# Linear attention and MLP on one core: the denominators, numerators and spreads of batch 1 a slot sooner, and two matmuls moved ahead of a spread

## Chip, cores and metric

One core of one Trainium2 chip. The metric is the device time of one execution in microseconds. "Before" and "changed" are the two kernels.

## The reference, cut

```python
# q, k, v: (8 batches, 8 heads, 576 positions, 64), float32
phi = lambda x: np.where(x > 0, x, np.exp(x) - 1.0) + 1.0
kv  = einsum('bhsd,bhse->bhde', phi(k), v);  z = phi(k).sum(axis=2)
num = einsum('bhsd,bhde->bhse', phi(q), kv)
den = einsum('bhsd,bhd->bhs', phi(q), z)[..., None] + 1e-06
x   = (num / den) as (4608 tokens, 512)
h   = x @ w_in                       # (512, 2048)
out = (h - tanh(h)) @ w_out          # (2048, 512)
```

## The kernel before

Products run in bf16 (the spreads of batch 0 in f32). The 4608 tokens pass through the two MLP products in nine chunks of 512; a batch has 576, so chunk 1 needs the last 64 tokens of batch 0 and 448 of batch 1. Attention of batch 1 is worked in between the matmuls of chunk 0. In chunk 0 the second product is cut into 16 "slots" of four 128x512 matmuls; `s2[n]` lists what is issued behind slot n. The denominators of a batch come out of TensorE as a small tile; VectorE inverts it (`rden`), splits it into bf16 parts (`a_split`), TensorE spreads it over partitions ("spread"), and VectorE multiplies the numerators with it ("scaling"), which gives `xT`, the input of the first product. The "kv matmuls" multiply k and v of a batch (line 177 for batch 1, line 199 for the later ones). One scaling makes one "pair" of heads, and each 128x512 matmul of the first product reads one pair.

```python
def a_scale(b, p, ns, bp, o):                        # a scaling of batch 1 (line 359 of the profile)
    nc.vector.tensor_mul(xT[:, p, S*b:S*b+S]..., ns[:, p]..., bp[:, :, o:o+144]...)
...
b0_spread((0, 2), 0)                                 # batch 0: first spread, banks 4 to 7
b0_scale(0, ns0, 0, 0, 4); b0_scale(0, ns0, 0, 4, 8) # pair 0 in halves (line 244)
b0_scale(2, ns0, 1)                                  # pair 2
b0_num(1, ns0)
def open2():
    b0_spread((1, 3), 2)                             # second spread, the same four banks
    b0_scale(1, ns0, 2); b0_scale(3, ns0, 3)
...
# chunk 0, slots of the second product
s2[4].append(lambda: (a_qphi(1, 1), load_q(2), load_k(2), load_v(2)))
s2[7].append(lambda: (a_qT_pe(1, 0, side), a_kv(1, side), a_qT_pe(1, 1, side)))
s2[8].append(lambda: b0_scale_rest(side))
s2[9].append(lambda: (a_den(1, side), num1(), a_split(1)))
s2[11].append(lambda: spread1(0))                    # 8 small matmuls and the scalings of pairs 0, 1
s2[11].append(lambda: (exp2(qs, q_t, qp_t, "qp", 0), rest2(qs[0])))
s2[12].append(lambda: exp2(qs, q_t, qp_t, "qp", 1))
s2[13].append(lambda: (spread1(1), exp2(ks, k_t, kp_t, "kp", 0), rest2(qs[1]), a_qT_dma(2)))
s2[14].append(lambda: rest2(ks[0]))
...
# chunk 0, first product: (pair, block) in the order of issue
order = [((0, 0), (0, 1)), ((2, 0), (2, 1), (0, 2), (0, 3), (2, 2), (2, 3)),
         [(p, fi) for p in (1, 3) for fi in range(4)]]
for n, part_ in enumerate(order):
    if n == 1:
        open2()
    ...
```

Behind slots 12 to 15 ScalarE copies one finished output bank each ("eviction", line 396), and the `exp2` calls put q's and k's exponentials of batch 2 on ScalarE among them.

## Time and profile before

| | before |
|---|---|
| median of 3 executions | 293.31 us (293.09 to 293.58) |
| span of the profiled one | 291.8 us |
| TensorE, VectorE, ScalarE busy | 98%, 60%, 48% |

TensorE is the bound, but the busy share cannot tell where it waits, since its durations overlap. What tells it is the distance between starts: 0.216 us from one 128x512 matmul to the next in a stream. A clearly longer distance is a wait, with two exceptions: where the tile shape of the matmul changes, 0.306 to 0.312 us is the distance without a wait; and 0.428 to 0.432 us, two beats, is taken for a record missing from the trace.

### The profile page before, as it was taken

What the parts mean: (1) busy time and instruction counts of PE and PEld (TensorE: products, weight loads), DVE (VectorE), ACT (ScalarE), POOL (GpSimd) and SP (SyncE); (2) the same over time, 40 slices, a digit from 0 to 9 for tenths busy, and PEclk for the clock granted to TensorE, in tenths of its full rate; (3) what the DMA queues carried; (4) which work ended last, traced back from release to release, by engine and by line L of the source; (5) the groups of instructions that cost most, each with busy time, mean ns of one, the idle gap of its engine ahead of it and who ended that gap; (6) DMA issues with size and microseconds to landing.
All of it is one profiled execution on the core that took longest, in us unless ns stands there. A gap on an engine that the chain in (4) does not pass through costs nothing.

```text
span 291.8 us, 4505 instructions
## 1 busy us (share of the span) xinstructions
PE 285.5 (98%) x1803; PEld 134.5 (46%) x1803; DVE 175.1 (60%) x266; ACT 139.7 (48%) x168; POOL 33.7 (12%) x56
## 2 busy tenths in 40 slices
PE   8999999999999999999999999999999999999994
PEld 3544464454454444444454444444544444444443
DVE  4759958987468674776478637865581457106600
ACT  4938548846354733465345534751551155126411
POOL 8674030110030003000300030000000000000000
PEclk9999999999999999999999999999999999999999
DMA  7999999997999768965895579666117310130032
GB/s 105 193 202 212 208 206 215 194 183 149 249 158 161 175 128 137 197 146 121 136 223 123 123 139 197 146 138 139 30 38 165 73 36 0 43 83 19 0 74 72
DMA packets 39093, 38.94 MB, mean 133 GB/s; under 512 B 16352, under 2 KB 33824, under 8 KB 38304
## 3 DMA queue, kind: packets, MB, share of 16 engines
q0 software_dynamic: 17568, 18.35, 39.0%
q1 hardware_dynamic: 21344, 20.17, 30.9%
q8 instruction: 14, 0.23, 0.3%
q10 hardware_dynamic: 160, 0.13, 0.1%
q14 instruction: 7, 0.06, 0.1%
HBM read 43.91 MB, written 9.55 MB: 183 GB/s over the span
## 4 chain that ended last, share of the span: by engine, by line
PE 85%; DMA 11%; POOL 2%; issue 1%; DVE 0%; POOLq 0%
PE ps_all L387 39%; PE ps_all L366 38%; DMA v<-in_v_dram 6%; DMA w_in_sb<-in_moe_w_in_dram 3%; PE ps_all L199 2%; DMA kraw<-in_k_dram 2%; PE ps_all L317 2%; PE ps_all L618 1%; PE ps_all L276 1%; POOL v L419 1%; PE ps_all L177 1%; POOL qraw L90 0%; PE ps_all L320 0%; POOL qraw L93 0%; POOL w_out_sb L115 0%
## 5 line engine op out<-in xcount | busy, mean ns | idle before, releaser
L366 PE MATMUL ps_all<-xT,w_in_sb 128*128 128x512 bf16 x574 | 127.6, 379 | 0.0
L387 PE MATMUL ps_all<-w_out_sb,gT 128*128 128x512 bf16 x560 | 127.5, 379 | 0.0
L373 DVE TENSOR_TENSOR gT<-ps_all,th 128x1024 bf16<-128x1024 f32 x64 | 77.9, 1218 | 59.2 <-ACT th L372 59.2
L372 ACT ACTIVATE th<-ps_all 128x1024 f32<-128x1024 f32 x64 | 65.6, 1025 | 57.1 <-PE ps_all L366 46.5
L366 PEld LDWEIGHTS <-w_in_sb 128*128 128x128 bf16 x574 | 55.0, 98 | 66.1 <-issue 0.3
L387 PEld LDWEIGHTS <-gT 128*128 128x128 bf16 x560 | 54.2, 98 | 64.2
L396 ACT COPY osb<-ps_all 128x512 f32<-128x512 f32 (+1 forms) x36 | 20.9, 583 | 71.8 <-PE ps_all L387 52.6
L328 DVE TENSOR_TENSOR xT<-ps_all,rdb 128x512 bf16<-128x512 f32 x24 | 16.5, 691 | 13.7 <-PE ps_all L317 11.2
L134 ACT ACTIVATE e<-qraw 128x1152 bf16<-128x1152 bf16 x16 | 18.5, 1160 | 8.2 <-DMA qraw<-in_q_dram 8.2
L134 ACT ACTIVATE e<-kraw 128x1152 bf16<-128x1152 bf16 x15 | 17.5, 1164 | 0.3 <-DMA kraw<-in_k_dram 0.3
L136 DVE TENSOR_TENSOR qp<-e,r 128x1152 bf16<-128x1152 bf16 x16 | 12.1, 758 | 8.0 <-ACT e L134 7.2
L136 DVE TENSOR_TENSOR kp<-e,r 128x1152 bf16<-128x1152 bf16 x15 | 11.4, 759 | 7.9 <-ACT e L134 6.9
L383 POOL COPY g<-qT 1x1 bf16<-1x1 bf16 x5 | 0.9, 178 | 119.2 <-DMA qT<-qp 119.2
L378 DVE TENSOR_TENSOR gT<-ps_all,th 128x512 bf16<-128x512 f32 x16 | 10.3, 686 | 2.4 <-ACT th L377 1.7
L377 ACT ACTIVATE th<-ps_all 128x512 f32<-128x512 f32 x16 | 9.2, 598 | 4.4 <-PE ps_all L366 3.2
L447 PE MATMUL ps_all<-zero 128*128 128x512 bf16 x29 | 9.2, 480 | 1.2 <-DVE zero L405 1.2
L317 PE MATMUL ps_all<-qT,kz 128*128 128x512 bf16 x28 | 10.1, 379 | 0.0
L135 DVE TENSOR_SCALAR r<-qraw 128x1152 bf16<-128x1152 bf16 x16 | 7.3, 454 | 2.1 <-DMA qraw<-in_q_dram 2.1
L199 PEld LDWEIGHTS <-kp 64*128 64x128 bf16 x216 | 6.4, 94 | 2.5 <-issue 2.1
L285 DVE RECIPROCAL rden<-den 128x144 f32<-128x144 f32 x7 | 7.4, 1053 | 0.2
L199 PE MATMUL ps_all<-vp,kp 64*128 64x136 bf16 x216 | 7.4, 220 | 0.0
L394 DVE COPY osb<-ps_all 128x128 f32<-128x128 f32 x1 | 0.3, 292 | 11.6 <-PE ps_all L618 11.6
(85 smaller groups left out, 123.6 us busy)
## 6 DMA issues: line engine op xcount, KB each, us to landing
out_dram<-osb SPq DMA_DIRECT2D x70, 128.0 KB
rdb<-ds SPq DMA_DIRECT2D x12, 576.0 KB
kraw<-in_k_dram POOLq DMA_DIRECT2D x7, 576.0 KB, 7.1
qraw<-in_q_dram POOLq DMA_DIRECT2D x7, 576.0 KB, 9.1
v<-in_v_dram POOLq DMA_DIRECT2D x7, 576.0 KB, 11.6
w_in_sb<-in_moe_w_in_dram POOLq DMA_DIRECT2D x6, 256.0 KB, 8.7
w_out_sb<-in_moe_w_out_dram POOLq DMA_DIRECT2D x3, 512.0 KB, 14.7
qraw<-in_q_dram POOLq DMA_DIRECT2D x2, 288.0 KB, 4.4
```

Source lines behind the costliest of these rows:

```text
L134: return (lambda: nc.scalar.activation(e, x, AF.Exp), lambda: nc.vector.tensor_scalar(r, x, 0.0, 1.0, ALU.max, ALU.add), lambda: nc.vector ...
L136: lambda: nc.vector.tensor_tensor(y, e, r, ALU.min))
L199: nc.tensor.matmul(ps[hg][:, i, :], kp[r, i, j].rearrange("p h d -> p (h d)"), vp[r, i, j, :], start=(j == 0), stop=(j == J - 1))
L317: nc.tensor.matmul(ps, kz[:, p // 2, p % 2, 0:128], qT[:, p % 2, 0:8, p // 2, :], start=True, stop=True)
L328: nc.vector.tensor_mul(xT[:, p, S * b:S * b + 512].rearrange("p (j t c) -> p j t c", j=8, t=4), ps.rearrange("p j (t c) -> p j t c", t=4), ...
L366: nc.tensor.matmul(h, w_in_sb[:, 2 * (p % 2) + p // 2, fi * 128:(fi + 1) * 128], xT[:, p, c * 512:(c + 1) * 512], start=(n == 0), stop=(n ...
L372: nc.scalar.activation(th, h, AF.Tanh)
L373: nc.vector.tensor_sub(gT[:, fi:fi + 2, :], h, th)
L377: nc.scalar.activation(th, h, AF.Tanh)
L378: nc.vector.tensor_sub(gT[:, fi, :], h, th)
L387: nc.tensor.matmul(o, gT[:, fi, i * 128:(i + 1) * 128], w_out_sb[:, fi, :], start=(fi == 0), stop=(fi == NF - 1))
L396: nc.scalar.copy(osb[:, f0:f1], o[:, f0:f1])
```

## The change

The intent: start the long VectorE chain of batch 1 (invert, split) and its spreads earlier, so that the scalings are done well ahead of chunk 1; and let TensorE do something useful ahead of the second spread of batch 0.

```diff
-            s2[8].append(lambda: b0_scale_rest(side))
-            s2[9].append(lambda: (a_den(1, side), num1(), a_split(1)))
-            s2[11].append(lambda: spread1(0))
+            s2[8].append(lambda: (b0_scale_rest(side), a_den(1, side), num1(), a_split(1)))
+            s2[10].append(lambda: spread1(0))
...
-            s2[11].append(lambda: (exp2(qs, q_t, qp_t, "qp", 0), rest2(qs[0])))
-            s2[12].append(lambda: exp2(qs, q_t, qp_t, "qp", 1))
-            s2[13].append(lambda: (spread1(1), exp2(ks, k_t, kp_t, "kp", 0), rest2(qs[1]), a_qT_dma(2)))
+            s2[11].append(lambda: exp2(qs, q_t, qp_t, "qp", 0))
+            s2[12].append(lambda: (spread1(1), exp2(qs, q_t, qp_t, "qp", 1), rest2(qs[0])))
+            s2[13].append(lambda: (exp2(ks, k_t, kp_t, "kp", 0), rest2(qs[1]), a_qT_dma(2)))
...
-            order = [((0, 0), (0, 1)), ((2, 0), (2, 1), (0, 2), (0, 3), (2, 2), (2, 3)),
+            order = [((0, 0), (0, 1)), ((2, 0), (2, 1)), ((0, 2), (0, 3), (2, 2), (2, 3)),
...
-                if n == 1:
+                if n == 2:
                     open2()
```

The last two edits are part A, the slots are part B.

## The prediction

> **What bounds the kernel now.** I read the page first, then the chain of work that ended last in order of time, then the timeline of each engine around the two places the diff touches (14 to 20 us and 38 to 53 us), and last the start of every matmul in the trace. From the page:
>
> ```profile
> span 291.8 us, 4505 instructions
> PE 285.5 (98%) x1803; PEld 134.5 (46%) x1803; DVE 175.1 (60%) x266; ACT 139.7 (48%) x168; POOL 33.7 (12%) x56
> PE 85%; DMA 11%; POOL 2%; issue 1%; DVE 0%; POOLq 0%
> ```
>
> TensorE is the bound: no other engine is over 60% busy, and the last chain is 85% TensorE. What this change can win is time in which TensorE stands still, not work. In the middle of the span a 128x512 matmul starts every 0.216 us (the durations of 379 ns in the page overlap). So I listed every start later than that: after 52.10 us there is none that waits, only fixed extra gaps of 0.095 us (start to start 0.309 to 0.312 us) where matmuls of another tile shape begin, alike in every batch. Whatever reaches 52.10 us sooner ends sooner, and whatever doesn't, doesn't. Between 17.68 us and 38.4 us TensorE keeps its 0.216 us beat with no wait. So the whole case is decided by a few waits, and by what ends each of them. From the chain, in order of time (start, length, what):
>
> ```profile
> 22.32 16.50 DMA v<-in_v_dram
> 38.83 0.04 issue
> 38.87 1.66 PE ps_all L177 x36
> ```
>
> The reader is to see that the path does not run through TensorE before 38.87 us: it runs through the load of v of batch 1, issued by GpSimd at 22.32 us and landing at 38.82. TensorE had started its last transpose at 38.427; 0.056 for it and 0.095 for the shape change make 38.58, so it stood 0.29 us for that load.
>
> The second place, ScalarE's timeline behind slot 11:
>
> ```profile
> 47.34 1.16 ACT L134 ACTIVATE e<-qraw 128x1152 bf16<-128x1152 bf16 x1 [1.40 <-DMA qraw<-in_q_dram]
> 48.41 0.57 ACT L396 COPY osb<-ps_all 128x512 f32<-128x512 f32 x1
> 48.87 1.16 ACT L134 ACTIVATE e<-qraw 128x1152 bf16<-128x1152 bf16 x1
> 49.94 0.57 ACT L396 COPY osb<-ps_all 128x512 f32<-128x512 f32 x1
> 50.40 1.17 ACT L134 ACTIVATE e<-kraw 128x1152 bf16<-128x1152 bf16 x1
> 51.47 1.07 ACT L396 COPY osb<-ps_all 128x512 f32<-128x512 f32 x2
> ```
>
> ScalarE sits idle 1.40 us until q of batch 2 lands (47.27), then works back to back through three exponentials and the evictions of output banks 0, 1, 2, 3. The eviction of bank 2 starts at 51.47 and ends at 52.05. The ninth matmul of chunk 1 writes that bank, and two narrow cuts of TensorE's timeline show it late:
>
> ```profile
> 51.75 0.38 PE L366 MATMUL ps_all<-xT,w_in_sb 128*128 128x512 bf16 x1
> 52.10 0.38 PE L366 MATMUL ps_all<-xT,w_in_sb 128*128 128x512 bf16 x1
> ```
>
> It starts 0.353 us after its neighbour (51.748 to 52.101) instead of 0.216: 0.137 us of wait, ended by ScalarE, whose time was set by a load.
>
> **What the Trainium skill says.** "PSUM — Partial Sum Buffer", section "PSUM bank collisions raise a hardware error", says accesses must be kept apart by bank and quadrant, not by address. The trace agrees: the second spread of batch 0 writes columns 256 and up of banks 4 to 7, VectorE reads columns below that, and still the spread starts at 17.02, just after VectorE's read of pair 2 ended (16.29 + 0.68 = 16.97). "TensorEngine Tiling (Array Packing)", section "Key Properties", says a change of tiling mode drains TensorE; the 0.095 us extra at each shape change here fits. "TensorE: Matmul & The Clock Gate", section "Back-to-back issue gap", gives N/2.4 + 2.5 ns for isolated matmuls, 216 ns at N = 512, and 131 ns sustained; this trace shows 216 in long streams, so I use 216.
>
> **The change, part A: two matmuls ahead of the second spread.** Nothing is added or removed. Before, TensorE ends the four 128x256 matmuls at 16.64 (last start 16.53 + 0.108) and stands until 17.02 for VectorE's scaling of pair 2. The matmuls (2,0) and (2,1) put there multiply xT of pair 2, which is the output of that same scaling: in the compiled order the wait has simply moved from the spread to matmul (2,0). They start at about 17.02 too and fill nothing. The spread then starts 2 x 0.216 later, plus about 0.1 for the shape change that used to lie inside the wait: 17.55. It takes 0.66 (17.02 to 17.68 before), so TensorE goes on at 18.21 with four matmuls and comes to pair 1 at 18.21 + 0.86 = 19.07. Pair 1 is scaled 1.55 us after the spread starts (before: 17.02 to 17.885 + 0.686 = 18.57), so at 19.10, seen at about 19.15. Before, pair 1 began at 18.985. Part A by itself costs 0 to 0.17 us; early loading of the spread's weights might give back 0.1. Either way it lies ahead of the 0.29 us wait for v at 38.87 and vanishes in it.
>
> **Part B: denominators, numerators and spreads a slot sooner.** In the compiled order one group of four 128x512 matmuls (4 x 0.216 = 0.864 us) moves from ahead of the denominators of batch 1 to behind the last spread. TensorE's work stays equal. From VectorE's timeline:
>
> ```profile
> 42.16 0.42 DVE L263 TENSOR_TENSOR xT<-ps_all,rdb 128x256 bf16<-128x256 f32 x1 [0.37 <-PE ps_all L320]
> 43.40 0.31 DVE L281 TENSOR_SCALAR den<-ps_all 128x144 f32<-128x144 f32 x1 [0.82 <-PE ps_all L276]
> 43.74 1.05 DVE L285 RECIPROCAL rden<-den 128x144 f32<-128x144 f32 x1
> 45.77 0.37 DVE L298 SCALAR_TENSOR_TENSOR w<-t,part,u 128x144 bf16<-128x144 bf16 x1
> ```
>
> From the addition at L281 to the end of w is 46.14 - 43.40 = 2.74 us, reciprocal and splitting included. Before, TensorE was ready for the first spread at 46.09 and got w at 46.195: 0.10 us of wait. After, the denominators' matmuls start at about 42.08 (42.91 - 0.864 + 0.03 for another shape change); VectorE is still in L263, so L281 starts at about 42.55, w is done at 45.29, and the spread can start at 45.35. TensorE arrives 8 matmuls after the numerators, about 43.44 + 1.73 + 0.095 = 45.27. So a wait of 0.08 remains, not zero, because the same eight matmuls lie between numerators and spread as before. Chunk 1 begins at about 50.24 + 0.02.
>
> What B does buy is slack: on VectorE, scalings of pairs 2 and 3 now stand ahead of the q work of batch 2 and end at about 49.3 rather than 50.62. But pair 3 is first needed at 50.885, so the 50.62 was already 0.26 us early. Then TensorE comes to bank 2 at about 51.98, and that bank is free at 52.05 as before: ScalarE's order of instructions is unchanged and its chain starts from a load whose issue (38.81, after the q work of batch 1) TensorE does not set. It starts at 52.10 in both kernels.
>
> **Sum.** A: at most +0.17, hidden by 0.29. B: +0.02, hidden by 0.137. After 52.10: 0. Expected difference 0.0 us, from 293.31 us. I take 293.2, a tenth lower, since other executions may have v and q land earlier, where a little of the sooner scalings could show.
>
> **The rivals.**
> 1. *The scalings were sometimes late.* Before, scalings 2 and 3 stood on VectorE behind work that waits for the q load; a later landing would stop TensorE at pair 3, and B removes that. Against: pair 3 follows the landing by 3.4 us (50.67 - 47.27), the bank 2 eviction by 4.8, and TensorE needs 1.1 us between the two, so the eviction is the later one in any case. Worth 0 to 0.3 us.
> 2. *Loads land sooner in most executions than in the profiled one.* Then neither wait hides anything, A's cost of up to 0.17 and B's 0.02 show, and the time is up to 293.5.
> 3. *A new wait in B:* numerator banks 6 and 7 are reused only 0.1 to 0.2 us after VectorE has read them (bank 7: read ends 42.86, next matmul at about 43.0). If VectorE is 0.2 late, TensorE is too: 0.1 to 0.2 us, mostly swallowed at 52.10.
> 4. *A real gain* of the size of the removed waits: 0.38 + 0.10 us, to 292.8. For it speaks only the intent; against it the two load-bound waits.
>
> **Range and chances.** Three executions before spread over 0.49 us (293.09 to 293.58), as landings vary. Taking rivals 2 and 4 as ends, 292.8 to 293.7. A change of 2% is 5.9 us; all of TensorE's idle time is 291.8 - 285.5 = 6.3 us, nearly all of it before the first matmuls and after the last. So within 2% is all but certain.
>
> **What would show it.** In the changed kernel's trace: matmul (2,0) starting at about 17.02 and the second spread after 17.4; the start of the kv matmuls of batch 1 still set by v's load near 38.9; the first spread near 45.35 with a small VectorE wait; the last two scalings of batch 1 done by 49.4; a late matmul near 52.1 behind the eviction of bank 2. The prediction is wrong if loads land elsewhere (a landing 1 us off moves the end by as much), or if chunk 1's ninth matmul no longer waits.

## The result

| | before | changed |
|---|---|---|
| median of 5 executions | 293.38 us (293.09 to 293.61) | 293.50 us (293.18 to 293.90) |
| ratio, 95% interval | | 1.0004 (0.9989 to 1.0018) |
| span of the profiled one | 291.8 us | 291.7 us |

A ratio is the mean time of one kernel's fast runs over that of the other's of the same rounds, so not quite the ratio of the medians. The time is the same within the noise, and inside the predicted range. From the changed kernel's page:

```profile
span 291.7 us, 4505 instructions
...
PE 285.7 (98%) x1803; PEld 134.8 (46%) x1803; DVE 174.9 (60%) x266; ACT 139.9 (48%) x168; POOL 33.8 (12%) x56
...
PE 90%; DMA 5%; POOL 1%; DVE 1%; ACT 1%; issue 1%; SPq 0%; DVEq 0%; POOLq 0%
```

The busy times say nothing. The chain that ended last does: DMA's share fell from 11% to 5%. Its pieces in order of time (start, length, what):

```profile
15.85 1.36 DVE xT L244 x3
17.21 0.04 issue
17.25 0.59 PE ps_all L366 x2
17.84 0.66 PE ps_all L240 x16
18.50 13.12 PE ps_all L366 x60
31.62 6.91 PE ps_all L387 x32
38.53 0.50 PE ps_all L164 x9
39.03 1.59 PE ps_all L177 x36
```

In this execution the path runs through TensorE without a break; the load of v of batch 1, which carried it before, is no longer in this stretch. v landed at 38.59 us, 0.37 us before TensorE came to the kv matmuls (L177, first start 38.962).

Part A, on TensorE's timeline (start, length, engine, line, operation, output and inputs, shape, count, and in brackets the idle time ahead with what ended it), before:

```profile
16.09 0.71 PE L580 MATMUL ps_all<-xT,w_in_sb 128*128 128x256 bf16 x4
...
17.02 0.73 PE L240 MATMUL ps_all<-rden,sel 32*128 32x128 f32 x16 [0.22 <-DVE xT L244]
...
17.68 8.59 PE L366 MATMUL ps_all<-xT,w_in_sb 128*128 128x512 bf16 x39
```

and changed:

```profile
17.25 0.59 PE L366 MATMUL ps_all<-xT,w_in_sb 128*128 128x512 bf16 x2 [0.22 <-DVE xT L244]
17.77 0.73 PE L240 MATMUL ps_all<-rden,sel 32*128 32x128 f32 x16
18.43 1.32 PE L366 MATMUL ps_all<-xT,w_in_sb 128*128 128x512 bf16 x5
```

The wait in brackets is the same 0.22 us, for the same VectorE scaling; it has moved from the spread to the two matmuls. Nothing was filled. VectorE's scalings of batch 0, before and changed:

```profile
15.62 1.35 DVE L244 TENSOR_TENSOR xT<-ns,ps_all 128x256 bf16<-128x256 f32 x3 [0.50 <-PE ps_all L240]
17.89 1.29 DVE L244 TENSOR_TENSOR xT<-ns,ps_all 128x512 bf16<-128x512 f32 x2 [0.92 <-PE ps_all L240]
```

```profile
15.85 1.35 DVE L244 TENSOR_TENSOR xT<-ns,ps_all 128x256 bf16<-128x256 f32 x3 [0.50 <-PE ps_all L240]
18.63 1.29 DVE L244 TENSOR_TENSOR xT<-ns,ps_all 128x512 bf16<-128x512 f32 x2 [1.44 <-PE ps_all L240]
```

VectorE now idles 1.44 us instead of 0.92 ahead of pairs 1 and 3, because the spread comes later.

Part B, VectorE's last two scalings of batch 1, before and changed:

```profile
49.21 1.41 DVE L359 TENSOR_TENSOR xT<-ns,ps_all 128x576 bf16<-128x576 f32 x2
```

```profile
47.85 1.42 DVE L359 TENSOR_TENSOR xT<-ns,ps_all 128x576 bf16<-128x576 f32 x2 [0.58 <-PE ps_all L354]
```

They end at 49.27 instead of 50.62 us, as intended. ScalarE's chain in the changed kernel:

```profile
46.58 1.16 ACT L134 ACTIVATE e<-qraw 128x1152 bf16<-128x1152 bf16 x1 [1.42 <-DMA qraw<-in_q_dram]
...
50.72 1.07 ACT L396 COPY osb<-ps_all 128x512 f32<-128x512 f32 x2
```

and chunk 1's matmuls on TensorE:

```profile
50.33 4.05 PE L366 MATMUL ps_all<-xT,w_in_sb 128*128 128x512 bf16 x18
```

q of batch 2 landed 0.75 us earlier than in the trace of before, so bank 2 was evicted by 51.30, and the ninth matmul of chunk 1 did not wait: it started at 52.055, 0.215 us after its neighbour.

**The ledger.** The start of one matmul can be compared between traces only as a distance from another, because the beginning itself jitters: the first scaling of batch 0 started at 15.62 us in one trace and 15.85 in the other, with nothing changed ahead of it. So I cut the span at five marks and compare the pieces:

| piece (us) | before | changed | difference |
|---|---|---|---|
| start to first scaling of batch 0 | 15.617 | 15.845 | +0.228 |
| to the first matmul of pair 1, chunk 0 (A) | 3.368 | 3.529 | +0.161 |
| to the first kv matmul of batch 1 (wait for v) | 19.885 | 19.588 | -0.297 |
| to the first matmul of chunk 1 (B) | 11.367 | 11.367 | 0.000 |
| to the first kv matmul of batch 2 (wait for bank 2) | 8.001 | 7.866 | -0.135 |
| to the end | 233.558 | 233.544 | -0.014 |
| sum | 291.796 | 291.739 | -0.057 |

One trace each: the second and fourth rows are the change, the first, third and fifth could be loads that landed differently. So the small sum does not show yet that A's 0.161 us was hidden. The experiments are to tell that.

### The profile page after: what moved, and what is told of

Same layout as the page of the kernel before. It is cut to its first block, busy times and chain, and to the rows that moved or that the text cites. A ratio compares the mean times of both kernels' runs of the same rounds, so it can differ in the third digit from the quotient of the medians.

```text
span 291.7 us, 4505 instructions
## 1 busy us (share of the span) xinstructions
PE 285.7 (98%) x1803; PEld 134.8 (46%) x1803; DVE 174.9 (60%) x266; ACT 139.9 (48%) x168; POOL 33.8 (12%) x56
## 4 chain that ended last, share of the span: by engine, by line
PE 90%; DMA 5%; POOL 1%; DVE 1%; ACT 1%; issue 1%; SPq 0%; DVEq 0%; POOLq 0%
PE ps_all L366 43%; PE ps_all L387 39%; DMA v<-in_v_dram 3%; DMA out_dram<-osb 2%; PE ps_all L199 2%; PE ps_all L317 2%; PE ps_all L276 1%; ACT osb L396 1%; PE ps_all L177 1%; POOL kraw L90 0%; PE ps_all L240 0%; SPq L401 0%; DVE xT L244 0%; POOL qraw L90 0%; PE ps_all L221 0%
```

## The experiments

Theory: part A costs 0.16 us on TensorE, part B nothing; the end is set by the later of TensorE's own work and two loads (v of batch 1 at the kv matmuls, q of batch 2 through the eviction of bank 2), so part of A is hidden, and B's slack lies where nothing waits. Rivals: B gains what A loses; or A pays. Runs of one group shared a chip and the runs of before.

### Part A alone

```diff
-            order = [((0, 0), (0, 1)), ((2, 0), (2, 1), (0, 2), (0, 3), (2, 2), (2, 3)),
+            order = [((0, 0), (0, 1)), ((2, 0), (2, 1)), ((0, 2), (0, 3), (2, 2), (2, 3)),
-                if n == 1:
+                if n == 2:
```

> Part A alone (two matmuls of pair 2 ahead of the second spread of batch 0), the slots as before. My theory: in the trace pair 1's first matmul of chunk 0 starts 0.1 to 0.2 us later, counted from the first scaling of batch 0 (before 18.985 - 15.617 = 3.37 us, here 3.5 to 3.55), with a small VectorE wait; at the end 0.0 to +0.2 us, according to how much of it the wait for v of batch 1 hides. Rival 'A pays': the same distance shrinks by up to 0.38 us and the time falls by 0.1 to 0.4 us.

Measured: median 293.53 us (before in these rounds 293.50), ratio 1.0000 (0.9988 to 1.0013). First scaling to pair 1: 3.529 us, to the nanosecond the changed kernel's. The wait for v in this trace was 0.30 us (0.450 between starts less the 0.152 that the last transpose and the shape change need). A loses 0.161 us; "A pays" falls.

### Part B alone

The slots of the changed kernel, with `order` and `open2` as before.

> Part B alone (denominators, numerators and spreads a slot sooner), the order of chunk 0 as before. My theory: from the first kv matmul of batch 1 to the first matmul of chunk 1 TensorE needs 11.37 us as before, within 0.05, a wait of about 0.1 us before the first spread stays; time within 0.2 us of before. Rival 'B gains what A loses': this distance shrinks by 0.1 to 0.2 us, and this kernel is 0.1 to 0.3 us faster than before and than the changed one.

Measured: median 293.28 us, ratio 0.9993 (0.9980 to 1.0005). From kv to chunk 1 11.368 us, as before (11.367). "B gains what A loses" falls on that distance. The end of the chain on VectorE's timeline and the spread on TensorE's show why the wait for `w` stays:

```profile
44.64 0.37 DVE L298 SCALAR_TENSOR_TENSOR w<-t,part,u 128x144 bf16<-128x144 bf16 x1
```

```profile
45.06 0.30 PE L354 MATMUL ps_all<-w,sel 32*128 32x144 bf16 x8
```

`w` is ready at 45.01 and the spread starts at 45.06, 0.417 us after the matmul ahead of it (before: 0.415). Both ends moved by the same slot, so the wait between them (0.417 less 0.312) is the same 0.10 us.

### Before and changed once more

Both kernels unedited, as a control and for second traces.

> The kernel before, unchanged, as a control and for a second trace. All theories: ratio 1.000 within 0.002. My theory of the loads: when v of batch 1 lands after the last transpose of the first half of q of batch 1, TensorE stands; in this trace that wait is somewhere between 0 and 0.5 us, the distances on TensorE between the waits are the same as in the first trace within 0.02 us.

> The changed kernel, unchanged, for a second trace and on the same chip as the control. All theories: within 0.2% of before. My theory: distance from the first scaling of batch 0 to pair 1's first matmul again 3.53 us (before 3.37), from the first kv matmul to chunk 1 again 11.37 us.

Measured: before again 293.49 us, ratio 0.9995 (0.9982 to 1.0007); changed again 293.51, ratio 0.9999 (0.9985 to 1.0013). So the noise of such a comparison is some 0.13%, 0.38 us, more than A costs: only the distances inside the traces can settle this. They repeat: first scaling to pair 1 3.369 and 3.529 us, kv to chunk 1 11.367 and 11.368. What does not repeat is the loads: the wait at the kv matmuls was 0.26 us in the second trace of before and 0.14 in that of the changed kernel, the wait for bank 2 0 and 0.19. In the first pair it was the other way round for bank 2 (0.14 before, none changed). So the fifth row of the ledger does not follow the change: the wait at bank 2 comes and goes in both kernels. The third row, the wait for v, depends both on when v lands and on how late TensorE arrives.

### Part A made larger

```diff
-            order = [((0, 0), (0, 1)), ((2, 0), (2, 1), (0, 2), (0, 3), (2, 2), (2, 3)),
+            order = [((0, 0), (0, 1)), ((2, 0), (2, 1), (0, 2), (0, 3), (2, 2), (2, 3)), (),
-                if n == 1:
+                if n == 2:
```

> Part A made larger: all six matmuls (two of pair 2, four more) ahead of the second spread, the rest as before. My theory: the spread starts 4 matmuls later than in part A, 0.87 us, and pair 1 waits for its scaling; scaling 0 to pair 1's first matmul is 3.529 + 0.865 = 4.39 us (before 3.37), so 1.03 us lost there; 0.15 to 0.3 us of it is hidden by the wait for v; the end is 0.6 to 1.0 us later, ratio 1.002 to 1.0035. Rival 'the loads hide it': the wait for v takes it up wholly and the time stays within 0.2 us. Rival 'A pays': the distance stays below 3.37.

Measured: median 294.20 us against 293.35, ratio 1.0035 (1.0022 to 1.0049), that is about 1.0 us slower. First scaling to pair 1: 4.393 us, 1.03 more than before, where 4.39 was expected. (One matmul record ahead of it is missing in this trace; the time is read from the matmul's own record.)

```profile
18.32 0.73 PE L240 MATMUL ps_all<-rden,sel 32*128 32x128 f32 x16
19.93 0.59 PE L366 MATMUL ps_all<-xT,w_in_sb 128*128 128x512 bf16 x2 [0.88 <-DVE xT L244]
```

TensorE runs out of work behind the spread and waits 0.88 us for the scaling of pair 1. This is what A does in small: every matmul put ahead of the spread delays the spread, and the spread's scaling is what TensorE needs next. There was no wait for v in this trace; a loss larger than the hiding place reaches the end.

### v sooner, in both kernels

```diff
+    load_v(1)
     for i in (1, 0):
         nc.gpsimd.memset(v_b[i][:, 2], 1.0)
     nc.gpsimd.memset(vp[:, :, :, 128:136], 1.0)
-    load_v(1)
```

> The order before, but the load of v of batch 1 issued ahead of GpSimd's three memsets, 2.3 us sooner. My theory: the kv matmuls follow the last transpose after 0.152 us (0.41 to 0.44 in the two traces of before), the end is 0.2 to 0.3 us sooner, unless q of batch 1 lands later for it and its transposes wait instead. Rival 'v is not the limit': the end does not move.

> The changed kernel with the same early load of v. My theory: with the wait for v gone part A's 0.161 us is no longer hidden: kv matmuls 0.15 us later, counted from the first scaling of batch 0, than in the kernel before with the early v, and the end 0.0 to 0.2 us later than there. Rival 'A costs nothing': equal.

Measured: 293.49 us, ratio 1.0008 (0.9995 to 1.0020), and 293.65, ratio 1.0010 (0.9997 to 1.0022). A miss in both. The chain of the first:

```profile
12.15 8.64 DMA w_in_sb<-in_moe_w_in_dram
20.79 0.28 issue
21.08 17.65 DMA v<-in_v_dram
38.72 0.05 issue
38.77 1.66 PE ps_all L177 x36
```

The load was issued 1.2 us sooner than in the first trace of before (22.32), not 2.3, since GpSimd then waits for a piece of w_in to land; and it took 17.65 us instead of 16.50, so it landed at 38.72 instead of 38.82. The wait for v stayed (0.14 us). The landings in the traces show why an earlier issue did not help: in all 14 traces the loads that GpSimd issues landed in the order of their issue, and v 2.83 to 2.92 us behind q of batch 1 (q at 35.94 and v at 38.82 in the first trace of before, 35.82 and 38.72 here). The edit moved v's issue, but not its place in that line.

From the first scaling of batch 0 to the kv matmuls it was 23.107 us here and 23.118 in the changed kernel with the early v. That these agree does not show that A was hidden: here TensorE waited for v, there it did not wait at all, since v had landed 0.44 us before. Without any wait (where there was one, it is taken off) TensorE needs 22.96 us for this stretch with the order of before and 23.12 with A's, in every trace. So what counts is how long after the first scaling v lands. In A alone and the second trace of the changed kernel it was 23.37 and 23.21 us, and the wait for v hid A wholly; in the first trace of the changed kernel and with the early v 22.75 and 22.68, and A lay on the path whole (0.155 us there); in the changed kernel with late q, below, 22.95, and 0.12 us of it did.

### A version with three waits taken out

v early as above, and

```diff
-            s2[8].append(lambda: b0_scale_rest(side))
-            s2[9].append(lambda: (a_den(1, side), num1(), a_split(1)))
+            s2[8].append(lambda: (b0_scale_rest(side), a_den(1, side), num1(), a_split(1)))
-            s2[11].append(lambda: (exp2(qs, q_t, qp_t, "qp", 0), rest2(qs[0])))
+            s2[11].append(lambda: exp2(qs, q_t, qp_t, "qp", 0))
-            s2[13].append(lambda: (spread1(1), exp2(ks, ...), rest2(qs[1]), a_qT_dma(2)))
-            s2[14].append(lambda: rest2(ks[0]))
+            s2[13].append(lambda: (spread1(1), rest2(qs[0]), rest2(qs[1]), a_qT_dma(2)))
+            s2[15].append(lambda: (exp2(ks, k_t, kp_t, "kp", 0), rest2(ks[0])))
```

> A version that takes out the three waits that my theory names and keeps the order of chunk 0 of before: v early; denominators and numerators a slot sooner but the spreads in their old slots (0.10 us of wait for w gone); k's exponential of batch 2 behind the last eviction of chunk 0 (bank 2 free about 1.1 us sooner, 0 to 0.19 us of wait gone). My theory: from the first kv matmul to chunk 1 11.27 us (11.367 before), from chunk 1 to the next kv 7.866 us with no late matmul, and the end 0.3 to 0.5 us sooner than before, ratio 0.9983 to 0.999. Rival: a load of q or k takes the place of the waits and the time stays within 0.2 us.

Measured: 293.52 us, ratio 1.0003 (0.9991 to 1.0016). The wait for `w` is gone as expected: 11.261 us from kv to chunk 1, and the bank 2 wait too. But v landed at 39.06 and cost 0.31 us, and a new wait of 0.146 us appeared in chunk 1 at 57.42 us. The profile names no releaser for it; the matmul starts 0.05 us after VectorE's subtraction h - tanh(h) (line 373) ends at 57.37, which now stands behind the k work, so that is the likely cause, not a shown one. The waits were traded, not removed.

### q late on purpose, in both kernels

```diff
-            s2[4].append(lambda: (a_qphi(1, 1), load_q(2), load_k(2), load_v(2)))
+            s2[4].append(lambda: a_qphi(1, 1))
+            s2[7].append(lambda: (gate(qT_t[1]), load_q(2), load_k(2), load_v(2)))   # behind the transposes
```

> The kernel before with the loads of batch 2 held back by about 3.3 us on purpose (issued once q of batch 1 is transposed, near 42.1 instead of 38.8 us). My theory: the end moves by about the lateness less the slack, 2 to 3.3 us later; TensorE stops at pair 3 (and 2) of chunk 1 because scalings 2 and 3 stand behind q's work on VectorE, at about q's exponential + 3.34 us, and again at the ninth matmul, which starts at q's exponential + 4.77 us. Rival 'q is not on the path': the end moves by less than 0.3 us.

> The changed kernel with the same late loads. My theory: no stop at pairs 2 and 3 (the scalings stand ahead of q's work), but the stops move to the eviction of banks 0, 1 and 2 on ScalarE, the ninth matmul again at q's exponential + 4.77 us, and the end is within 0.3 us of the other late kernel. Rival 'the slack of B is worth its size': 0.3 to 0.6 us or more faster than the other late kernel.

`gate` is a small GpSimd instruction that reads the end of a tile, so that the loads behind it are issued only when that tile is written.

Measured: 294.27 us, ratio 1.0029 (1.0014 to 1.0044), and 294.18, ratio 1.0026 (1.0012 to 1.0040). The load was issued 3.4 us later but took less time, so q's exponential started only 0.5 to 1.4 us later than in the two plain traces of each kernel, and the end moved by 0.7 to 0.8 us, less than the 2 us that I expected at least. The mechanism is as expected. TensorE, before with late q:

```profile
51.28 1.24 PE L366 MATMUL ps_all<-xT,w_in_sb 128*128 128x512 bf16 x5 [0.29 <-DVE xT L359]
52.71 0.59 PE L366 MATMUL ps_all<-xT,w_in_sb 128*128 128x512 bf16 x2 [0.19 <-ACT osb L396]
```

and changed with late q:

```profile
51.23 0.38 PE L366 MATMUL ps_all<-xT,w_in_sb 128*128 128x512 bf16 x1
...
52.77 0.38 PE L366 MATMUL ps_all<-xT,w_in_sb 128*128 128x512 bf16 x1 [0.51 <-ACT osb L396]
```

In the kernel before, pair 3 waits for VectorE's scaling, which stands behind q's work, and then the ninth matmul for the eviction. In the changed one pair 3 does not wait, but the fifth matmul (51.23, 0.521 us after its neighbour) waits for bank 1, whose eviction ended at 51.18, and the ninth waits longer. The ninth starts 4.764 us after q's exponential in both (47.943 to 52.707, 48.004 to 52.768). B takes away a wait that a later one covers.

### The last load of w_out later, alone and with the denominators early

```diff
-    load_wo(3)
-            s1[13].append(lambda: a_kphi(1, 1))
+            s1[13].append(lambda: (a_kphi(1, 1), gate(kp_t[1]), load_wo(3)))
```

The second kernel has this and the denominators a slot sooner with the spreads in their old slots, as above, without the early v; k's exponential stays in slot 13.

> The kernel before with the last load of w_out (512 KB in the kernel's type) issued about 8 us later, after the k work of batch 1, so that it does not share the DMA engines with v of batch 1. My theory: v lands 0.5 us or more sooner, the kv matmuls follow the last transpose after 0.152 us, TensorE gains 0.15 to 0.3 us up to there; whether it lasts to the end depends on q of batch 2, which now has the w_out load beside it: end 0.3 us sooner to 0.2 us later. Rival 'v lands by its queue's order alone': the wait for v stays at 0.41 to 0.47.

> The same late load of w_out, with denominators and numerators a slot sooner but the spreads in their old slots, and the order of chunk 0 of before. My theory: from the first kv matmul to chunk 1 11.26 us, as in the version with the waits removed, kv after the transpose 0.152 us, the end 0.2 to 0.4 us sooner than before if q of batch 2 lands no later; otherwise the wait at bank 2 takes it, and the time stays within 0.2 us.

Measured: 293.41 us, ratio 0.9997 (0.9984 to 1.0009), and 293.31, ratio 0.9996 (0.9983 to 1.0008). A miss for v: the wait was 0.11 and 0.16 us, shorter than in the two traces of before (0.29, 0.26) but there, and v landed at about the same time as before (38.82 and 38.56; before 38.82 and 38.52). The edit did not do what it was meant to: issued at 33.40 (in the first of the two) instead of 24.55 us, the load of w_out landed at 43.87, before at 43.90. It stood behind v in the line of loads either way. The rival, that v lands by its queue's order alone, fits: v landed 2.91 and 2.90 us behind q of batch 1, as in the other traces. (Only the distance that this rival named, 0.41 to 0.47 us, was not met; it was 0.26 and 0.31.) In the second, kv to chunk 1 was 11.262 us as expected, 0.10 us won, and the ninth matmul then waited 0.27 us for bank 2: q's exponential started at 47.10 and the matmul at 51.86, 4.76 us later as in the other traces with this wait. No version beat both kernels beyond the noise.

### The distances side by side

One trace for each number, in us; "v landed" is counted from the first scaling of batch 0, "wait for v" is the distance to the kv matmuls' predecessor less 0.152, "bank 2" the excess over 0.216 at the ninth matmul of chunk 1.

| kernel | first scaling to pair 1 | v landed | wait for v | kv to chunk 1 | bank 2 |
|---|---|---|---|---|---|
| before, again | 3.368, 3.369 | 23.21, 23.17 | 0.29, 0.26 | 11.367, 11.367 | 0.14, 0 |
| changed, again | 3.529, 3.529 | 22.75, 23.21 | 0, 0.14 | 11.367, 11.368 | 0, 0.19 |
| A alone | 3.529 | 23.37 | 0.30 | 11.365 | 0 |
| B alone | 3.370 | 23.10 | 0.18 | 11.368 | 0.15 |
| A made larger | 4.393 | 23.11 | 0 | 11.367 | 0 |
| v early, before and changed | 3.371, 3.529 | 23.06, 22.68 | 0.14, 0 | 11.370, 11.371 | 0, 0 |
| w_out late | 3.369 | 23.03 | 0.11 | 11.368 | 0 |
| spreads in old slots, den early (three waits out, w_out late) | 3.369, 3.368 | 23.23, 23.07 | 0.31, 0.16 | 11.261, 11.262 | 0, 0.27 |

## Why the prediction was right

- **Part A costs 0 to 0.17 us.** Right: 0.161 us, and 3.529 us from first scaling to pair 1 in each trace with A's order. Both reasons held: the wait moved from the spread to the matmuls, and pair 1 then waits for its scaling (0.288 us between starts instead of 0.216). The 0.1 us that early loading of the spread's weights might have given back did not come.
- **A vanishes in the wait for v.** Half right. The wait exists and hides A where v lands late: in two of the five traces with A's order wholly, in one by a quarter, in two (the profiled execution among them) not at all. The prediction took 0.29 us from one trace; in the seven traces with the order of before and q not held back the wait was 0.11 to 0.31 (two of before, B alone, early v, the three waits taken out, and late w_out twice). The stated sign "the kv matmuls are still set by v's load" was therefore wrong for the profiled execution, and rival 2 described it. That the two profiled executions ended within 0.06 us of each other is luck of the landings: the changed one came to the kv matmuls 0.09 us later (38.962 against 38.870) and made that up at bank 2 (0.135 us), since q of batch 2 landed 0.75 us sooner.
- **Part B costs 0.02 us and leaves a wait of 0.08.** The distance changed by 0.000 us and the wait stayed at 0.10. The step that was off is the 0.03 us that I added for "another shape change": the matmuls of the denominators follow a 64-column matmul now, 0.123 us after it instead of 0.029, so the same 0.094 us as before.
- **The slack of B lies where nothing waits.** Right: the scalings ended at 49.27 (49.3 predicted), no time came of it, and with q late the eviction at 4.764 us after q's exponential ended the wait in both kernels.
- **The ninth matmul waits at 52.1 in both.** Wrong for the profiled execution: q landed 0.75 us sooner and it did not wait. Seen over the runs it comes and goes in both kernels with q's landing.
- **A tenth below the time before.** The wrong side: 293.50 us against 293.38, a difference within the noise. No single comparison resolves A's cost. Put together afterwards, within the rounds that they shared, the kernels with A's order (changed twice, A alone, changed with early v; 20 runs) were 0.14 us slower than those with the order of before (before, B alone, before with early v; 38 runs), with a 95% interval of about 0.02 to 0.25. That is an estimate, and takes B and the early v for worth nothing; it fits an A that is hidden in some executions and not in others. What stays open is why the landing of the whole line of loads moves from one execution to the next.

## What to carry to other kernels

Before work is moved ahead of a waiting instruction to fill its wait, ask what that work itself waits for: here it was the same scaling, so the wait only changed its place, and the delayed instruction fed the next consumer late. Moving a producer and its consumer by the same number of slots leaves the wait between them as it was; only moving one of them changes it. And where the noise of whole executions is larger than the effect, cut the trace at marks and compare the distances: they repeated within 0.006 us here while the times of one kernel moved by up to 0.9 us in one group of runs. Last, a distance that ends in a wait for a load compares landings, not code: count the landing from the same mark before calling a cost hidden. And issuing a load sooner moved its landing nowhere here, since its place in the line of loads stayed; another place in the line was not tried.

## What the Trainium skill lacked or had wrong

- "TensorE: Matmul & The Clock Gate", section "Back-to-back issue gap", gives 131 ns per matmul at N = 512 as the sustained rate of weight load and matmul pairs. In long streams here it was 0.215 to 0.216 us in every trace, the page's figure for the isolated gap.
- "TensorEngine Tiling (Array Packing)", section "Key Properties", says that a change of tiling mode drains TensorE but not what that costs. Here it was 0.09 to 0.10 us at each change behind a 128x512 matmul (0.306 to 0.312 against 0.216 us; behind a 64-column matmul 0.123 against 0.029).
- No page that I read says how far the landing of one load varies between executions of one program: q's exponential of batch 2, which starts as q lands, began at 46.58 and 47.51 us in the two traces of the changed kernel, and the first scaling of batch 0 between 15.35 and 15.85 us in the four traces of before and changed.
